# One more token-tile pair by seven half-size products in the first FFN, with the softmax steps set closer

## The chip, the cores and the metric

The kernel runs on one core of one Trainium2 chip. The metric is device time in microseconds, median of several runs. TensorE (PE) multiplies, VectorE (DVE) and ScalarE (ACT) work on SBUF and PSUM, GpSimd (POOL) on SBUF, SyncE (SP) issues every DMA.

## The reference

Attention over keys and values pooled by eight, then two feed-forward networks on 4608 tokens. All in float32.

```python
def _attn_ref(q, k, v):                        # 8 batches, 8 heads, 576 tokens, 64 wide
    k_p = k.reshape(B, H, Sp, pool, D).mean(axis=3)     # Sp = 72
    v_p = v.reshape(B, H, Sp, pool, D).mean(axis=3)
    scores = scale * np.matmul(q, k_p.transpose(0, 1, 3, 2))
    scores = scores - np.max(scores, axis=-1, keepdims=True)
    attn = np.exp(scores)
    attn = attn / (np.sum(attn, axis=-1, keepdims=True) + 1e-09)
    return np.matmul(attn, v_p)

def _moe_ref(x, w_in, w_out):                  # x: 4608 x 512, w_in: 512 x 2048
    h = x @ w_in
    return np.maximum(0.01 * h, h) @ w_out

def _moe2_ref(x, w_gate, w_val, w_out, rms_g): # 512 x 1536
    rms = np.sqrt(np.mean(x * x, axis=-1, keepdims=True) + 1e-06)
    xn = x / rms * rms_g
    g = xn @ w_gate
    return (g / (1.0 + np.exp(-g)) * (xn @ w_val)) @ w_out
```

## The kernel before

**Numbers.** Every factor of a large product is kept as a high and a low part, and a product is three matmuls (high by high, high by low, low by high). A result in PSUM is therefore read twice on its way to SBUF: ACT copies the high part, DVE or POOL subtracts it for the low part.

**Order.** Each engine executes its instructions in the order of the program text: at the end the kernel ties each instruction to the one before it on its engine. So the text is the schedule, and SP's queue of DMAs is one list too.

**Token tiles.** The 4608 tokens are nine tiles of 512. `PLAIN` of them, seven, go through the first FFN plainly: for each of 16 blocks f, `h_half` computes x@w_in in two chunks of six matmuls (192 matmuls in a tile); after the second chunk ACT applies the leaky ReLU twice (`h_high`) and DVE subtracts (`h_low`); two blocks later `y_unit` multiplies with w_out in two more chunks. From the third block on the chunks go h, h, y, y. A tile has 64 chunks, called stages here. Tile 0 has a hand-written order (`FIRST`) in which the attention of the first two batches and the preparation of the weights are laid out; its last 28 chunks are stages 0 to 27, tile 1 begins with stage 28.

**The pair.** The last two tiles are a pair: x@w_in goes by seven half-size products instead of eight (Strassen and Winograd's form; `Quad`, eight quads of seven products of six matmuls, `kinds` 1). Its operands are sums of halves of w_in, prepared earlier and stored to DRAM ("h" units), and of halves of x, made by `token_steps` from x in DRAM. Pieces of the product with w_out run between the products. The second FFN goes by pairs of the same kind throughout (`kinds` 2).

**Softmax steps.** After each chunk `attention_point` runs what `late_attention` put at that stage. Query tile i (batch b, tile t of five; the fifth has 64 new rows, the others 128) starts at `start[i]`. Its chain, and what stands behind it on the other engines:

```python
stage("s", b, t, (s, s, s + 1, s + 1, s + 3, s + 4))
stage("r", b, t, (s + 6,))
stage("x", b, t, (s + 7,) * 3)
stage("y", b, t, (s + 8,) * 3)
if i + 1 < len(tiles):
    stage("t", *tiles[i + 1], (s + 6,) * 2)
```

"s" is the scores in two halves (L322, tile `sc`; at s and s+1), on DVE their maximum and the subtraction (L335, L336), the exponential on ACT at s+3, the normalization on DVE at s+4 (last: L346). "x" transposes the exponentials (L383, `xt`), ACT copies the high part (L387), DVE subtracts (L389, `at`). "y" does so for the remainder that doesn't fill 128 rows (L397, `xr`; L401; L404, `atr`), "t" transposes the next queries (L302, `qt`). Transposes, scores and the products with v (`av`, L426, two stages behind the second and the fifth tile of a batch, one head pair per stage) share two PSUM banks, tag "att", handed out in turn. Within a stage what an earlier query tile put comes first.

**Where the output goes.** `step_av` writes the attention output of a plain tile to SBUF as high and low parts; that of the paired tiles is copied on ACT (L452, `xs`) and stored to DRAM two stages later. A chunk of 256 or 320 tokens that crosses a tile edge takes two copies.

**Side units.** The operands for the pairs and for the second FFN are built by units placed at stages (`side_steps`: 16 "h" units every `H_STEPS` stages from `SIDE_BEGIN` on, then gate, value and output units until `SIDE_END`); those left over run in the pair, one tick after each product or piece.

Of the kernel before, what the change touches and what calls it, by code (L numbers as in the profile page):

```python
# [9 lines left out]
F32 = mybir.dt.float32  # L10
# [13 lines left out]
def pooled_attention_then_two_ffns(  # L24
# [27 lines left out]
    N = 512  # L52
    NJ = NT // N
    begun = len(nc.cur_bb.bb.instructions)
    PLAIN = NJ - 2
    H_STEPS, G_STEPS, P_STEPS, SIDE_BEGIN, SIDE_END = 4, 11, 9, 84, 356
    QT = [0, 128, 256, 384, S - P]
    RB = [0, 128, 256, 384, H * SP - P]
    CH = [(0, 256, (0, 1)), (256, S, (2, 3, 4))]
# [350 lines left out]

    def x_tile(j):
        if j not in xhl:
            if j in (3, 6):
                xhl[j] = [weight_slot(9 + 2 * c, f"xhl{j}_{c}") for c in range(KC)]
            else:
                t = per.tile([P, 2, KC, N], F32R, tag="xhl", bufs=2, name=f"xhl{j}")
                xhl[j] = [t[:, :, c, :] for c in range(KC)]
        return xhl[j]
# [89 lines left out]
    def late_attention():  # L508

        def put(point, f):  # L510
            at_point.setdefault(point, []).append(f)

        def stage(kind, b, t, points):
            for point in points:
                put(point, lambda: go(kind, b, t))
            if kind in use:
                def free():
                    live["q" if kind == "t" else "kv"] -= 1
                put(points[0] + 3, free)

        start = {}
        for i in range(FIRST_LATE, len(tiles) + 1):
            start[i] = 34 + round(10.5 * (i - 10)) if i < 26 else 202 + 9 * (i - 26)
        for r, point in enumerate((4, 9, 14, 29, 31)):
            stage("kp", 2, r, (point,))
        stage("kt", 2, 0, (28,) * 2)
        stage("kt", 2, 1, (34,) * 2)
        stage("t", 2, 0, (28,) * 2)
        for i in range(FIRST_LATE, len(tiles)):
            b, t = tiles[i]  # L530
            s, after = start[i], start[i + 1]
# [6 lines that stand above are left out]
            if t < 2:  # L538
                for k in range(3):
                    stage("vp", b, 3 * t + k, (s + 2 * k,) * 2 + (s + 2 * k + 2,) * 2)  # L540
            if t in (2, 3) and b + 1 < B:
                for k in range(3 if t == 2 else 2):
                    stage("kp", b + 1, 3 * (t - 2) + k, (s + 4 * (t - 2) + 2 * k,))
                stage("kt", b + 1, t - 2, (after + 3,) * 2)
            if t in (1, 4):
                for p in range(NP):
                    stage(f"av{t // 4}", b, p, (after + 2 + p,) * 3)

    point_now = [0]
# [28 lines left out]
    for at_, (m, f) in enumerate(needs):  # L578
        src = rows(w_out, f) if m == "o" else cols(w_in, f)
        n = 2 * f + (m == "o")  # L580
# [3 lines left out]
    late_end = max(at_point) + 1  # L584
# [393 lines left out]
    def pair_loads(q):  # L978

        n = pairs[q][1]  # L980
        xs = [[None] * KC for _ in range(2)]

        def load(z, k):
            x = slot("u", 8 + 2 * z + k, f"xst{q}_{z}_{k}").bitcast(F32)
            j = pairs[q][0] // N + z
            nc.sync.dma_start(out=x, in_=x_dram[j][:, 2 * k:2 * k + 2, :])
            for c in range(2):
                xs[z][2 * k + c] = x[:, c, :]

        return xs, [lambda z=z, k=k: load(z, k) for z in range(2) for k in range(2)]  # L990
# [69 lines left out]
    def token_steps(q, xs, fine):  # L1060

        n = pairs[q][1]
        if kinds[q] == 2:
            xs = [[x[:, c, :] for c in range(KC)] for x in xs]
        t = tok[q] = {}
        box = {}
        done = [0]

        def parts(dst, src):
            done[0] += 1  # L1070
            split(nc.scalar, dst[:, HI, :], nc.gpsimd if done[0] % 3 == 0 else nc.vector, dst[:, LO, :], src)

        def sub(out, u, w):
            nc.vector.tensor_tensor(out=out, in0=u, in1=w, op=ALU.subtract)

        def first(c):
            if c == 0:
                box["a"] = per.tile([P, 2, KC, N], F32R, tag="xhl", bufs=2, name=f"xa{q}")
            t["B11", c] = box["a"][:, :, c, :n]
            t["B21", c] = box["a"][:, :, 2 + c, :n]  # L1080
            parts(t["B11", c], xs[0][c])

        def t_slot(name, c):
            i = {"T2": 0, "T1": 2, "T3": 4}[name] + c
            t[name, c] = slot("t", i, f"{name}_{q}_{c}")[:, :, :n]
            return t[name, c]

        def sums(c):
            a1, a2, b1, b2 = (xs[z][i] for z in range(2) for i in (c, 2 + c))
            for x in ("T3", "T2"):  # L1090
                box[x, c] = e_tile(n, f"{x}_{q}_{c}") if kinds[q] == 1 else (
                    per.tile([P, N], F32, tag="tg", bufs=3, name=f"{x}_{q}_{c}")[:, :n]
                )
            t3, t2 = box["T3", c], box["T2", c]
            sub(t3, b2, b1)
            sub(b1, b1, a1)
            sub(t2, b2, b1)

        def second(c):
            parts(t_slot("T2", c), box["T2", c])  # L1100
            parts(t_slot("T1", c), xs[1][c])

        def second_more(c):
            a2 = xs[0][2 + c]
            parts(t["B21", c], a2)
            parts(t_slot("T3", c), box["T3", c])
            sub(a2, a2, box["T2", c])

        def third(c):
            if c == 0:  # L1110
                box["b"] = per.tile([P, 2, KC, N], F32R, tag="xhl", bufs=2, name=f"xb{q}")
            t["T4", c] = box["b"][:, :, 2 + c, :n]
            t["B22", c] = box["b"][:, :, c, :n]
            parts(t["T4", c], xs[0][2 + c])
            parts(t["B22", c], xs[1][2 + c])

        def all_second(c):
            for f in (sums, second, second_more):
                f(c)

        two = (0, 1)
        early = [lambda c=c: first(c) for c in two]
        for c in two:
            early += [lambda c=c, f=f: f(c) for f in ((sums, second, second_more) if fine else (all_second,))]
        return early, [lambda c=c: third(c) for c in two]
# [70 lines left out]
    def first_pair(put):  # L1196
# [4 lines left out]
            put(i, x)  # L1201
        for i, x in zip((25, 27, 29, 31, 33, 36, 38, 41), early):
            put(i, x)
        for i, x in zip((44, 47), late):
            put(i, x)
        for i in (34, 36, 39, 41, 42, 44, 46, 48, 50, 52):
            put(i, load_a)
# [6 lines left out]
    def e_tile(n, name):  # L1214
        return p2.tile([P, N], F32, tag="e", bufs=9, name=name)[:, :n]
# [254 lines left out]
    n = 0  # L1470
# [10 lines left out]
    for j in range(1, PLAIN):  # L1481
        at_spot = {}
        last = j == PLAIN - 1
        if last:
            assert point_now[0] >= late_end
            begin_phase2()

        def put(i, x):
            at_spot.setdefault(i, []).append(x)
# [27 lines left out]
        if not last:  # L1517
            y_store(j)


    def piece():
        if pieces:
# [172 lines left out]
```

## Time and profile before

| | |
|---|---|
| median of 3 runs | 1790.53 us (1787.62 to 1790.8) |
| profiled execution | 1790.44 us, its span 1788.7 us |
| mean granted TensorE clock | 0.995 |
| PE busy | 1745.8 us, 98% of the span, 8488 matmuls |
| DVE, ACT, POOL busy | 913.4, 705.4, 624.6 us |
| tile 0, from the span's start | to about 169 us |
| plain tiles 1 to 5 | 169.02 to 705.91 us |
| plain tile 6 | 705.91 to about 787 us |
| the pair's products of x@w_in | 787.51 to 910.43 us |

Busy time of PE is the time between a matmul's start and its modelled end, which overlaps the next start: PE's pace is read from starts, and its waits from the gaps, which come out somewhat short. PEld is the weight load ahead of a matmul; a wait for a semaphore stands on it.

### The profile page before, as it was taken

What the parts mean: (1) busy time and instruction counts of PE and PEld (TensorE: products, weight loads), DVE (VectorE), ACT (ScalarE), POOL (GpSimd) and SP (SyncE); (2) the same over time, 40 slices, a digit from 0 to 9 for tenths busy, and PEclk for the clock granted to TensorE, in tenths of its full rate; (3) what the DMA queues carried; (4) which work ended last, traced back from release to release, by engine and by line L of the source; (5) the groups of instructions that cost most, each with busy time, mean ns of one, the idle gap of its engine ahead of it and who ended that gap; (6) DMA issues with size and microseconds to landing.
All of it is one profiled execution on the core that took longest, in us unless ns stands there. A gap on an engine that the chain in (4) does not pass through costs nothing.

```text
span 1788.7 us, 23981 instructions
## 1 busy us (share of the span) xinstructions
PE 1745.8 (98%) x8488; PEld 1484.2 (83%) x8488; DVE 913.4 (51%) x1610; ACT 705.4 (39%) x1512; POOL 624.6 (35%) x773
## 2 busy tenths in 40 slices
PE   5799999999999999999999999999999999999999
PEld 4689888888888888888788888999788889978887
DVE  7984447664655652335665445345534534553331
ACT  5664334454454543335453332243233223322220
POOL 5631317552434311114345332243144215413320
PEclk9899999999999999999999999999999999999999
DMA  8542655656566655659997656777765668676552
GB/s 250 184 154 96 250 193 182 192 181 209 165 213 204 188 155 176 202 182 381 311 311 256 217 197 227 238 278 251 256 235 195 216 225 302 241 256 212 181 209 93
DMA packets 203639, 387.46 MB, mean 217 GB/s; under 512 B 57216, under 2 KB 108416, under 8 KB 203008
## 3 DMA queue, kind: packets, MB, share of 16 engines
q1 hardware_dynamic: 203520, 385.94, 63.8%
q8 instruction: 67, 1.10, 0.3%
q14 instruction: 52, 0.43, 0.1%
HBM read 311.43 MB, written 74.45 MB: 216 GB/s over the span
## 4 chain that ended last, share of the span: by engine, by line
PE 89%; DVE 4%; DMA 3%; ACT 1%; issue 1%; POOL 1%; SPq 1%; ACTq 0%; POOLq 0%; DVEq 0%
PE o L1363 16%; PE y L641 16%; PE h L596 15%; PE yg L1235 6%; PE yv L1235 6%; PE o L1343 4%; PE xg L1235 4%; PE xv L1235 4%; PE wg L1235 4%; PE wv L1235 4%; PE sc L322 2%; PE yh L1235 1%; PE av L426 1%; PE wh L1235 1%; PE xh L1235 1%
## 5 line engine op out<-in xcount | busy, mean ns | idle before, releaser
L596 PE MATMUL h<-xhl,w_i 128*128 128x512 f32 (+1 forms) x1380 | 345.4, 393 | 8.0 <-DVE ghl L619 5.7
L1363 PE MATMUL o<-wo,u 128*128 128x512 f32 x1296 | 316.3, 392 | 3.1 <-DMA wo<-wo 3.0
L596 PEld LDWEIGHTS h<-xhl,w_i 128*128 128x128 f32 x1380 | 247.8, 190 | 53.1 <-DVE ghl L619 6.2
L1363 PEld LDWEIGHTS o<-wo,u 128*128 128x128 f32 x1296 | 243.3, 189 | 52.5 <-DMA wo<-wo 3.8
L619 DVE TENSOR_TENSOR ghl<-h,ghl 128x512 fp32r<-128x512 f32 (+1 forms) x115 | 77.8, 676 | 203.1 <-ACT h L101 197.1
L641 PE MATMUL y<-ghl,w_o 128*128 128x512 f32 (+1 forms) x864 | 174.3, 349 | 0.0
L641 PE MATMUL y<-ghl,wr 128*128 128x512 f32 x672 | 171.6, 397 | 0.0
L641 PEld LDWEIGHTS y<-ghl,w_o 128*128 128x128 f32 x864 | 136.5, 191 | 17.0
L641 PEld LDWEIGHTS y<-ghl,wr 128*128 128x128 f32 x672 | 122.4, 188 | 22.8
L101 ACT ACTIVATE ghl<-h 128x512 fp32r<-128x512 f32 (+1 forms) x115 | 67.4, 586 | 183.5 <-PE h L596 178.9
L98 POOL TENSOR_TENSOR u<-e2g,u 128x512 fp32r<-128x512 f32 (+1 forms) x25 | 29.6, 1184 | 304.9 <-ACT u L95 304.9
L1235 PE MATMUL yg<-T,ag 128*128 128x512 f32 (+1 forms) x360 | 84.0, 368 | 0.0
L1235 PE MATMUL yv<-T,av 128*128 128x512 f32 (+1 forms) x360 | 83.8, 368 | 0.0
L1235 PE MATMUL xg<-xa,ag 128*128 128x512 f32 (+1 forms) x360 | 83.8, 367 | 0.0
L1235 PE MATMUL xv<-xa,av 128*128 128x512 f32 (+1 forms) x360 | 83.7, 367 | 0.0
L1235 PEld LDWEIGHTS yg<-T,ag 128*128 128x128 f32 x360 | 66.0, 188 | 10.0 <-DVE e1v L1212 0.6
L1235 PEld LDWEIGHTS yv<-T,av 128*128 128x128 f32 x360 | 66.2, 188 | 9.5
L1235 PEld LDWEIGHTS xv<-xa,av 128*128 128x128 f32 x360 | 66.0, 188 | 9.5
L1235 PEld LDWEIGHTS xg<-xa,ag 128*128 128x128 f32 x360 | 66.1, 188 | 9.3
L228 POOL TENSOR_TENSOR v<-v 128x256 f32<-128x256 f32 (+1 forms) x96 | 63.6, 663 | 13.7 <-DMA v<-in_v_dram 10.0
L101 ACT ACTIVATE h<-h 128x512 f32<-128x512 f32 (+1 forms) x115 | 67.0, 582 | 0.0
L95 ACT ACTIVATE u<-e2g 128x512 fp32r<-128x512 f32 (+1 forms) x30 | 17.7, 590 | 120.6 <-DVE e2g L1266 120.6
(204 smaller groups left out, 3134.9 us busy)
## 6 DMA issues: line engine op xcount, KB each, us to landing
wo<-wo SPq DMA_DIRECT2D x148, 512.0 KB
ag<-op_g SPq DMA_DIRECT2D x90, 512.0 KB
av<-op_v SPq DMA_DIRECT2D x90, 512.0 KB
wr<-wo SPq DMA_DIRECT2D x56, 512.0 KB
k<-in_k_dram SPq DMA_DIRECT2D x40, 256.0 KB
q<-in_q_dram SPq DMA_DIRECT2D x40, 256.0 KB
op_g<-parts_g SPq DMA_DIRECT2D x36, 256.0 KB
op_v<-parts_v SPq DMA_DIRECT2D x36, 256.0 KB
```

Of the source, the lines that this page charges most:

```text
L95: nc.scalar.activation(out=hi, in_=src, func=AF.Copy)
L98: lo_eng.tensor_tensor(out=lo, in0=src, in1=hi.bitcast(F32), op=ALU.subtract)
L101: return nc.scalar.activation(out=out, in_=in_, func=AF.Prelu, scale=scale, alpha=alpha)
L228: nc.gpsimd.tensor_tensor(out=x[:, :n], in0=x[:, :n], in1=x[:, n:2 * n], op=ALU.add)
L322: nc.tensor.matmul(pt[:, i * n:(i + 1) * n], y[:, p, :], kblk[b % 2][:, p * n:(p + 1) * n], start=True, stop=True,)
L426: nc.tensor.matmul(pt[:, :n], vb[b, p][:, sp].rearrange("p h d -> p (h d)"), a[:, p, mp, 0:n], start=i == 0, stop=False,)
L596: nc.tensor.matmul(pt, w[:, sp, c * P:(c + 1) * P], x[c][:, mp, c0:c1], start=c == 0 and i == 0, stop=c == KC - 1 and i == 2,)
L619: nc.vector.tensor_tensor(out=t[:, LO, :], in0=pt, in1=t[:, HI, :].bitcast(F32), op=ALU.subtract)
L641: nc.tensor.matmul(pt, w[:, sp, m * P:(m + 1) * P], g[:, mp, a - c0:a - c0 + n], start=ydone[j, a] == 1 and i == 0 and m % per_bank == 0, ...
L1235: nc.tensor.matmul(pt, wt[:, a, c, sp, :], xt[:, mp, :], start=start and c == 0 and i == 0, stop=c == 1 and i == 2, skip_group_check=not s ...
L1343: nc.tensor.matmul(pt, w[:, sp, m * P:(m + 1) * P], u[:, mp, :], start=f == blocks(q, z)[0] and i == 0, stop=f == blocks(q, z)[-1] and i == 2,
L1363: nc.tensor.matmul(pt, u[:, sp, m * P:(m + 1) * P], w[:, mp, :], start=f == 0 and i == 0, stop=f == F2 - 1 and i == 2,)
```

## The change

The plain tiles become five (`PLAIN = NJ - 4`), and tiles 5 to 8 two pairs. The loop over `pairs` and `kinds` makes two pairs of kind 1 from that without further edits. Softmax steps now start every 7.9 stages, rounded: 26 of the 29 distances are 8, three are 7 (from (3,0), (4,4) and (7,0)); the last step's chain ends at stage 276 of 280. The h units come every six stages, the tile stages take 21 side units instead of 36, and 31 instead of 16 run in the pairs. x of the second pair is loaded into other slots; tile 4's x lies where tile 1's lay, so the splits that need the first pair's second x buffer stand at stages 58 and 59 of tile 4; two sums of the first pair use another pool, since the second phase's pool opens only behind the last plain tile.

```diff
--- before.py
+++ after.py
@@ -52,8 +52,8 @@
     N = 512
     NJ = NT // N
     begun = len(nc.cur_bb.bb.instructions)
-    PLAIN = NJ - 2
-    H_STEPS, G_STEPS, P_STEPS, SIDE_BEGIN, SIDE_END = 4, 11, 9, 84, 356
+    PLAIN = NJ - 4
+    H_STEPS, G_STEPS, P_STEPS, SIDE_BEGIN, SIDE_END = 6, 11, 9, 84, 228
     QT = [0, 128, 256, 384, S - P]
     RB = [0, 128, 256, 384, H * SP - P]
     CH = [(0, 256, (0, 1)), (256, S, (2, 3, 4))]
@@ -410,7 +410,7 @@
 
     def x_tile(j):
         if j not in xhl:
-            if j in (3, 6):
+            if j == 3:
                 xhl[j] = [weight_slot(9 + 2 * c, f"xhl{j}_{c}") for c in range(KC)]
             else:
                 t = per.tile([P, 2, KC, N], F32R, tag="xhl", bufs=2, name=f"xhl{j}")
@@ -520,7 +520,7 @@
 
         start = {}
         for i in range(FIRST_LATE, len(tiles) + 1):
-            start[i] = 34 + round(10.5 * (i - 10)) if i < 26 else 202 + 9 * (i - 26)
+            start[i] = 34 + round(7.9 * (i - 10))
         for r, point in enumerate((4, 9, 14, 29, 31)):
             stage("kp", 2, r, (point,))
         stage("kt", 2, 0, (28,) * 2)
@@ -981,7 +981,7 @@
         xs = [[None] * KC for _ in range(2)]
 
         def load(z, k):
-            x = slot("u", 8 + 2 * z + k, f"xst{q}_{z}_{k}").bitcast(F32)
+            x = slot("u", (6, 7, 2, 3)[2 * z + k] if q else 8 + 2 * z + k, f"xst{q}_{z}_{k}").bitcast(F32)
             j = pairs[q][0] // N + z
             nc.sync.dma_start(out=x, in_=x_dram[j][:, 2 * k:2 * k + 2, :])
             for c in range(2):
@@ -1088,7 +1088,7 @@
         def sums(c):
             a1, a2, b1, b2 = (xs[z][i] for z in range(2) for i in (c, 2 + c))
             for x in ("T3", "T2"):
-                box[x, c] = e_tile(n, f"{x}_{q}_{c}") if kinds[q] == 1 else (
+                box[x, c] = e_tile(n, f"{x}_{q}_{c}") if kinds[q] == 1 and q else (
                     per.tile([P, N], F32, tag="tg", bufs=3, name=f"{x}_{q}_{c}")[:, :n]
                 )
             t3, t2 = box["T3", c], box["T2", c]
@@ -1201,7 +1201,7 @@
             put(i, x)
         for i, x in zip((25, 27, 29, 31, 33, 36, 38, 41), early):
             put(i, x)
-        for i, x in zip((44, 47), late):
+        for i, x in zip((58, 59), late):
             put(i, x)
         for i in (34, 36, 39, 41, 42, 44, 46, 48, 50, 52):
             put(i, load_a)
@@ -1481,9 +1481,6 @@
     for j in range(1, PLAIN):
         at_spot = {}
         last = j == PLAIN - 1
-        if last:
-            assert point_now[0] >= late_end
-            begin_phase2()
 
         def put(i, x):
             at_spot.setdefault(i, []).append(x)
@@ -1518,6 +1515,9 @@
             y_store(j)
 
 
+    assert point_now[0] >= late_end
+    begin_phase2()
+
     def piece():
         if pieces:
             pieces.pop(0)()
```

## Rows read from the trace of the kernel before

**Rows 1.** The page's first part: busy time, share of the span, instructions of each engine.

```profile
PE 1745.8 (98%) x8488; PEld 1484.2 (83%) x8488; DVE 913.4 (51%) x1610; ACT 705.4 (39%) x1512; POOL 624.6 (35%) x773
```

**Rows 2.** Windows: us; busy PE, PEld, DVE, ACT, POOL (count); granted clock; DMA share; GB/s.

```profile
169.02:705.91 536.89, 534.04 (x2684) 445.92 (x2683) 289.64 (x629) 243.67 (x615) 208.50 (x353) 1.00 0.60 196
274.37:381.98 107.61, 106.34 (x532) 88.07 (x531) 73.67 (x167) 50.12 (x121) 69.19 (x103) 1.00 0.65 199
...
705.91:787.51 81.60, 81.60 (x361) 67.59 (x360) 28.22 (x42) 28.65 (x56) 10.63 (x12) 1.00 0.59 195
787.51:910.43 122.92, 120.47 (x527) 98.44 (x526) 69.88 (x124) 59.65 (x120) 42.98 (x49) 1.00 0.89 313
```

**Rows 3.** Timeline of PE in the pair: start, us, engine, line, operation, names, shapes, count.

```profile
848.70 1.52 PE L1235 MATMUL xh<-xa,ah 128*128 128x512 f32 x6
...
854.14 1.52 PE L1235 MATMUL yh<-T,ah 128*128 128x512 f32 x6
```

**Rows 4.** Timeline around the step of query tile (6,2), in tile 4.

```profile
566.08 0.60 PE L383 MATMUL xt<-ident,ex 128*128 128x128 f32 x4
...
567.40 0.69 DVE L389 TENSOR_TENSOR at<-xt,at 128x512 fp32r<-128x512 f32 x1 [2.75 <-ACT at L387]
...
568.05 1.64 PE L596 MATMUL h<-xhl,w_i 128*128 128x512 f32 x6
...
569.52 0.66 PE L322 MATMUL sc<-kblk,qT 128*128 128x144 f32 x4
...
569.92 1.41 PE L641 MATMUL y<-ghl,wr 128*128 128x512 f32 x5
```

**Rows 5.** Timeline around the step of query tile (6,3), in tile 4.

```profile
580.66 1.02 DVE L346 TENSOR_TENSOR ex<-ex,st 128x576 f32<-128x576 f32 x1
...
581.83 0.63 PE L383 MATMUL xt<-ident,ex 128*128 128x128 f32 x4 [0.74 <-DVE ex L346]
...
583.17 0.69 DVE L389 TENSOR_TENSOR at<-xt,at 128x512 fp32r<-128x512 f32 x1 [1.49 <-ACT at L387]
...
583.83 1.64 PE L641 MATMUL y<-ghl,w_o 128*128 128x512 f32 x6
...
585.30 0.66 PE L322 MATMUL sc<-kblk,qT 128*128 128x144 f32 x4
...
585.73 0.42 DVE L404 TENSOR_TENSOR atr<-xr,atr 32x256 fp32r<-32x256 f32 x1
```

**Rows 6.** Timeline around the step of query tile (6,0), in tile 4.

```profile
537.09 0.68 DVE L389 TENSOR_TENSOR at<-xt,at 128x512 fp32r<-128x512 f32 x1
...
537.13 1.63 PE L641 MATMUL y<-ghl,wr 128*128 128x512 f32 x6
```

**Rows 7.** Timeline of DVE at the scores of (6,3).

```profile
573.13 0.46 DVE L336 TENSOR_TENSOR ex<-sc,st 128x288 f32<-128x288 f32 x1
```

**Rows 8.** Waits of PE in tile 0 (36 to 169 us): total, times, longest.

```profile
PE av L426 <- DVE at L389: 2.7, 1, 2.7
...
PE sc L322 <- DVE at L389: 0.6, 1, 0.6
```

**Rows 9.** Waits of PE in tiles 1 to 5, longest total first.

```profile
PE xt L383 <- DVE ex L346: 1.2, 3, 0.7
```

**Rows 10.** Timeline where batch 7 crosses the edge of tiles 7 and 8.

```profile
639.37 1.56 PE L641 MATMUL y<-ghl,wr 128*128 128x512 f32 x6
640.95 0.46 ACT L452 COPY xs<-av 128x64 f32<-128x64 f32 x2 [4.67 <-DMA x<-xs]
...
641.46 0.62 PE L426 MATMUL av<-at,vb 128*128 128x256 f32 x3 [0.54 <-ACT xs L452]
```

**Rows 11.** Waits of PE in the pair's quads (787.51 to 910.43 us).

```profile
PE ms L1035 <- ACT ahl L95: 1.5, 1, 1.5
PE yh L1235 <- DVE e7h L1212: 0.6, 1, 0.6
```

**Rows 12.** Windows in the second FFN, columns as in rows 2.

```profile
1580.00:1590.00 10.00, 7.83 (x28) 5.99 (x27) 7.64 (x10) 4.95 (x10) 3.70 (x3) 0.83 0.70 226
```

## The prediction

> **What bounds the kernel now.** First the page's busy line: TensorE (PE) is busy 1745.8 of 1788.7 us, VectorE (DVE) 51%, ScalarE (ACT) 39%, GpSimd (POOL) 35% [rows 1]. Then the windows by token tile, since a share over the whole span hides stages: tiles 1 to 5 take 536.89 us, of which PE idles 2.85, and tile 6, without softmax work, not at all [rows 2]. So PE sets the time of the stretch that the change touches, and only two things can move it: how many matmuls PE runs, and how often it waits in its program order for another engine. For the pace, tile 6's 360 matmuls of 512 columns in 81.60 us are 226.7 ns each (the window counts one that hangs over) [rows 2].
>
> **What is removed.** Two plain tiles run 2 x 192 matmuls of x@w_in; the pair that exists now runs 56 half-size products of six, 336, at the same pace: 24 matmuls start between 848.70 and 854.14 [rows 3]. Nothing else on PE changes: the second product keeps 2 x 192, the softmax its transposes and scores. One more pair is therefore 48 matmuls less, 48 x 226.7 ns = 10.88 us. Of all terms this one is sure.
>
> **What is squeezed, as throughput.** The softmax of 30 query tiles is spread over five plain tiles now and must fit into four, about 536.89 - 384 x 0.2267 = 449.8 us. Even if all work of the other engines in the five tiles came along, DVE would be at 289.64/449.8 = 64%, ACT at 54%, POOL at 46%. Tile 2 runs today with DVE at 73.67/107.61 = 68% and PE idle 1.3 us [rows 2]. The side units only ease it (the h units come every six stages instead of four, 15 units move into the pairs). So no engine becomes the bound by its sum, and I cost density itself at nothing; what PE pays is single waits.
>
> **What is squeezed, as distance.** A step of query tile i starts at stage s; the transposes of its exponentials (xt) stand at s+7, those of their remainder (xr) at s+8, the scores of tile i+1 at the next s, in two halves a stage apart. All of them, and the query transposes (qt, at s+6), take turns in the two "att" banks in the order qt, xt, xr, scores 1, scores 2. So scores 1 reuse the bank of xt and wait for its last reader, the DVE subtraction of line 389. Steps are 9 to 11 stages apart now and 8 (three times 7) after. At 9, two chunks of six matmuls lie between xt and scores 1; at 8 only one.
>
> In an ordinary step xt ends at 566.68 and the subtraction at 567.40 + 0.69 = 568.09. Scores 1 come at 569.52 now; at a distance of 8 they are due right behind xr, where the next chunk starts now, at 568.05 [rows 4]. A release takes 0.15 us more (a normalization ends at 581.68, the transposes that waited for it start at 581.83 [rows 5]). They start at 568.24, 0.19 late. Eleven full-width steps, (5,0) to (5,3), (6,0) to (6,3) and (7,1) to (7,3), will lie so: 2.1 us.
>
> Where the chunk ahead of xt ends an h block, its two PReLUs go first on ACT and its own subtraction first on DVE. Then line 389 ends at 537.77 where the scores would be due at 537.13 [rows 6]: with the release 0.79 late. Steps that start at stages 34 to 58 fall so (s+7 is the second half of an h block): four full-width ones, 3.2 us.
>
> From stage 81 to 137 it is xr that stands behind the PReLUs, and scores 2 reuse its bank. In such a step, where xr stands just ahead of the chunk at 583.83, its subtraction ends at 586.15. At a distance of 8 scores 1 are due at 583.83 and, by line 389 (583.17 + 0.69), start 0.18 late; scores 2 are due one score group (0.40, as behind 569.52) and one chunk (1.47) later, at 585.88, and start at 586.30: 0.42 late [rows 4, 5]. Seven such steps at 0.60, and (3,4), whose narrow transposes leave only the second wait, 0.4: 4.6 us.
>
> Three steps are 7 apart. There scores 2 reuse the bank of scores 1, whose two DVE operations (0.46 each [rows 7]) stand behind line 389: 1.41 + 0.92 + 0.15 after xt against some 1.75 due, 0.7 late, and up to 0.8 more behind PReLUs. Estimate 3.0 together, 1 to 4.5. The narrow fifth tiles (2,4), (5,4) and (6,4) I take as free.
>
> Sum 12.9 us. No row of tiles 1 to 5 shows this wait; the nearest are in tile 0, where scores waited 0.6 and a product 2.7 us for the same subtraction [rows 8]. So a single wait lies between 0 and 2.7; I take the values above because they come from today's own end times.
>
> **Other terms.** (a) Stages 81 to 145 also put an h block's subtraction ahead of the normalization, which then ends just before xt, once 0.74 us too late [rows 5]. Steps in that position go from five to nine; today's waits there sum to 1.2 us [rows 9], so +1.0 (0 to 3). (b) Attention output of tiles 5 and 6 now goes to DRAM and back. Where a chunk of tokens crosses a tile edge, the copies of the second head pair wait on ACT until the first pair's stores have landed: ACT stood 4.67 us, and PE's next product, due 1.36 us after 639.37, came at 641.46, 0.73 late [rows 10]. One such crossing now, three after: +1.5 (0 to 9.3, if all of ACT's wait reached PE). (c) The new pair repeats the pair's wait for a sum: +0.6 [rows 11]. Its norm waits stay with the pair ahead of the second FFN. (d) The loads of x, the splits at stages 58 and 59 (needed seven products and pieces, about 9 us, later) and the late units are covered: the pair keeps one late unit per 8 or 5 ticks, as now, and PE never waits for DMA there at a DMA share of 0.89 [rows 2, 11]. If that cover fails, the nearest price is an idle stretch in the second FFN: 2.2 of 10 us, and 1.7 more, since the granted clock was 0.83 over them [rows 12].
>
> That also bears on the waits above: idle stretches of 0.7 and 1.5 us left the granted clock at 1.00 [rows 2, 5, 11], and the one of 2.2 us brought a stretch at the lower level (1.2 of 2.4 GHz). So I add nothing for the clock. The Trainium skill (TensorE: Matmul & The Clock Gate, A second HAM failure mode: psum-queue depth-cycling) has it otherwise: small idles from cycling through PSUM banks can come so often that the clock swings between its levels. By that rule the sum would grow by the rival below; by the rows it does not.
>
> **Total.** 1790.44 (profiled execution; the median of the runs is 1790.53) - 10.88 + 12.9 + 1.0 + 1.5 + 0.6 = **1795.6 us**, 0.3% slower.
>
> **Rivals.** *The gain stands.* If the scratch banks don't bind, only (a) to (c) remain: 1790.44 - 10.88 + 3.1 = 1782.7. It decides whether line 389 ends within 1.2 us of xt; it takes 1.41 today, so a small misreading decides much. For it: PE waits for no score in tiles 1 to 5. Against it: the distances there are longer by a chunk or more. *It cancels.* The waits of 0.19 and 0.18 vanish (3.4 us), (a) and (b) cost nothing, the longer ones remain: 16.0 - 5.9 = 10.1 against 10.88, 1789.7. *The clock follows.* If the seven or so longest waits (behind PReLUs, at distance 7) each bring a stretch at the lower level, 1.7 us each, 12 more: 1808. Against it: the idles that did not. The skill's section named above is what speaks for it. *The queues pile up*: the pair's sums, splits and loads fall into tile 4 beside softmax work; the forecast's upper end, to 1802.
>
> **Chances.** What a measurement of this kernel can tell from no change is about 0.2%, 3.6 us. The forecast with its own range, 1794 to 1802: 0.48; clock or DMA beyond it: 0.04; it cancels (1787 to 1794): 0.28; the gain stands (1780 to 1787): 0.20. So slower 0.52, same 0.28, faster 0.20. Leaving out the clock and most of the gaining case gives a range of 1783 to 1802.
>
> **What would show it.** The two pairs' x@w_in should run 336 matmuls each, at 227 ns. In tiles 1 to 4 the PE waits should have scores waiting for DVE "at" (line 389) and, from stage 81 to 145, for "atr" (line 404), in nearly every step, with a PE idle of some 15 us in four tiles where five had 2.85; "av" should wait for ACT "xs" three times; the clock should stay at 1.00. The forecast is wrong if those tiles show PE idle under 6 us: then the bank order or the release time was misread. If they show it and the time still falls, the pairs gave back more than 48 matmuls.

## The result and the profile after

The changed kernel takes 1814.31 us (median of four runs, 1813.02 to 1816.15), the kernel before 1790.66 beside it: ratio 1.0134, 95% interval 1.0117 to 1.0152, 1.3% slower. The profiled execution has a span of 1812.9 us against 1788.7, 24.2 more, where the sum had 5.1.

The page's busy line and the windows by stage of the changed kernel (columns as in [rows 2]): tiles 1 to 4, the first pair's quads, its second half, and the second pair.

```profile
PE 1748.3 (96%) x8440; PEld 1480.3 (82%) x8440; DVE 937.2 (52%) x1633; ACT 720.8 (40%) x1539; POOL 650.6 (36%) x797
```

```profile
169.06:284.99 115.93, 111.98 (x571) 92.64 (x569) 55.08 (x119) 46.86 (x125) 43.40 (x88) 1.00 0.60 213
284.99:408.33 123.34, 117.73 (x592) 95.85 (x591) 71.56 (x167) 54.18 (x141) 58.23 (x95) 0.99 0.52 159
408.33:524.41 116.08, 114.50 (x594) 95.44 (x593) 67.11 (x144) 56.21 (x145) 55.08 (x97) 1.00 0.64 201
524.41:637.34 112.93, 105.92 (x528) 87.67 (x526) 59.05 (x112) 52.74 (x131) 24.73 (x41) 0.98 0.58 186
637.34:755.79 118.45, 118.41 (x523) 97.74 (x521) 55.03 (x107) 52.96 (x109) 37.03 (x47) 1.00 0.91 307
755.79:810.44 54.65, 48.68 (x201) 39.10 (x200) 34.49 (x45) 24.31 (x49) 26.48 (x23) 0.94 0.86 304
810.44:978.00 167.56, 164.26 (x722) 134.99 (x721) 107.07 (x171) 85.83 (x171) 75.23 (x78) 1.00 0.89 304
```

PE runs 48 matmuls less, 8440 for 8488 [rows 1], so the gain of 10.9 us is there, and it is lost more than three times over. Six tiles took 618.49 us before [rows 2]; two of them at 384 x 226.7 ns are 174.1, which would leave 444.4 for four. They take 468.28 (169.06 to 637.34): **23.9 us lost** where the sum had 15.4. The pair before took 167.79 (787.51 to 955.30), and one more at the pace of its matmuls is 720 x 0.2267 = 163.2; the two take 173.10 + 167.56: **9.7 us lost**, nearly all in the first pair's second half, where the sum had 0.6. The second FFN behind them takes 1.5 more. 23.9 + 9.7 + 1.5 - 10.9 = 24.2.

PE idles 18.15 us in tiles 1 to 4, 2.85 in tiles 1 to 5 before [rows 2]. Its waits there (total, times, longest), to be held against [rows 9]:

```profile
PE sc L322 <- DVE at L389: 9.4, 12, 2.7
PE xt L383 <- ACT xs L452: 3.1, 2, 2.8
PE xt L383 <- DVE ex L346: 1.8, 3, 0.9
PE qt L302 <- ACT xs L452: 0.9, 1, 0.9
PE sc L322 <- DVE ex L336: 0.9, 2, 0.5
PE av L426 <- ACT xs L452: 0.7, 1, 0.7
```

The wait that no row of before's tiles showed, scores for the subtraction of line 389, is now the first. One of the twelve, from the timeline of the changed kernel in tile 1 (step of query tile (2,0)):

```profile
190.64 0.60 PE L383 MATMUL xt<-ident,ex 128*128 128x128 f32 x4
...
190.90 0.60 ACT L101 ACTIVATE ghl<-h 128x512 fp32r<-128x512 f32 x1 [0.66 <-PE h L596]
...
191.39 0.59 ACT L101 ACTIVATE h<-h 128x512 f32<-128x512 f32 x1
...
191.91 0.59 ACT L387 ACTIVATE at<-xt 128x512 fp32r<-128x512 f32 x1
192.02 0.69 DVE L619 TENSOR_TENSOR ghl<-h,ghl 128x512 fp32r<-128x512 f32 x1 [1.20 <-ACT h L101]
...
192.62 0.68 DVE L389 TENSOR_TENSOR at<-xt,at 128x512 fp32r<-128x512 f32 x1
...
193.36 0.76 PE L322 MATMUL sc<-kblk,qT 128*128 128x144 f32 x4 [0.51 <-DVE at L389]
```

The h block that ends ahead of xt puts two PReLUs (L101) ahead of the copy L387 on ACT and L619 ahead of L389 on DVE. L389 ends at 193.30, 2.0 us behind xt; the scores, one chunk and the remainder behind xt, wait for it. In a step without PReLUs the same pair ends 1.4 us behind xt. Seven of the twelve waits stand behind PReLUs in this way, 2.9 of the 9.4 us. At the other five, 6.4 us, side work stands ahead of L389 on ACT or DVE: a unit's conversion or the preparation of v (waits of 1.19, 2.70 and 0.75 us, at 280.66, 357.23 and 575.21) and the first pair's token sums (0.83 and 0.96 us, at 597.02 and 611.32; at 597.02 an h block's subtraction too). DVE ahead of the last one:

```profile
608.70 1.36 DVE L98 TENSOR_TENSOR T<-T,T 128x512 fp32r<-128x512 f32 x1 [0.37 <-ACT T L95]
...
609.99 0.68 DVE L1074 TENSOR_TENSOR xst<-xst,T 128x512 f32<-128x512 f32 x1
610.59 0.68 DVE L389 TENSOR_TENSOR at<-xt,at 128x512 fp32r<-128x512 f32 x1
```

The longest waits, PE's rows at four places of the timeline:

```profile
357.23 1.33 PE L322 MATMUL sc<-kblk,qT 128*128 128x144 f32 x4 [2.70 <-DVE at L389]
...
592.42 1.12 PE L383 MATMUL xt<-ident,ex 128*128 128x128 f32 x4 [2.78 <-ACT xs L452]
...
777.66 1.62 PE L1343 MATMUL o<-ug,wo 128*128 128x512 f32 x3 [3.80 <-DMA wo<-wo]
...
807.80 2.80 PE L1343 MATMUL o<-ug,wo 128*128 128x512 f32 x11 [1.42 <-POOL ug L98]
```

and what the clock did behind the first three, with the end of the first pair as the fourth row (windows):

```profile
357.20:361.00 3.80, 3.77 (x15) 3.30 (x15) 3.33 (x8) 0.63 (x1) 3.64 (x7) 0.61 0.45 125
592.40:596.00 3.60, 3.58 (x12) 2.89 (x12) 2.58 (x3) 3.33 (x8) 1.33 (x1) 0.54 0.08 27
777.60:784.00 6.40, 6.34 (x16) 5.04 (x17) 0.12 (x1) 0.78 (x2) 0.83 (x2) 0.54 1.04 412
795.00:810.44 15.44, 13.28 (x58) 10.33 (x57) 14.67 (x14) 7.77 (x16) 12.43 (x10) 1.00 0.72 243
```

Each of the three is followed by a stretch at or near the lower level (1.2 of 2.4 GHz). At a granted clock of 0.61 a stretch of 3.80 us does the work of 2.32, so it costs 1.5 us; the others 1.7 and 2.9: by this estimate about 6 us in all, 3 of them in the tiles. It is an upper bound: in runs 3, 4 and 12 below the same wait in tile 2 (2.69 us) left the clock at 1.00, and tile 2 takes only 0.6 to 0.8 us less (122.72, 122.71 and 122.58 for 123.34). In the fourth row DVE is busy 14.67 of 15.44 us: the next pair's token splits and the late units meet there, and ug comes late.

At 592.42 the cause is an edge crossing. ACT's wait for stores in tiles 1 to 4:

```profile
ACT xs L452 <- DMA x<-xs: 17.8, 10, 4.9
```

### The profile page after: what moved, and what is told of

Read it like the earlier page. It is cut to its first block, busy times and chain, and to the rows that moved or that the text cites. A ratio compares the mean times of both kernels' runs of the same rounds, so it can differ in the third digit from the quotient of the medians.

```text
span 1812.9 us, 24130 instructions
## 1 busy us (share of the span) xinstructions
PE 1748.3 (96%) x8440; PEld 1480.3 (82%) x8440; DVE 937.2 (52%) x1633; ACT 720.8 (40%) x1539; POOL 650.6 (36%) x797
## 4 chain that ended last, share of the span: by engine, by line
PE 79%; DVE 7%; DMA 5%; ACT 3%; issue 3%; POOL 1%; SPq 1%; POOLq 0%; ACTq 0%; DVEq 0%
PE o L1363 16%; PE h L596 8%; PE y L641 8%; PE o L1343 7%; PE yg L1235 6%; PE yv L1235 6%; PE xg L1235 4%; PE xv L1235 4%; PE wg L1235 4%; PE wv L1235 4%; PE yh L1235 3%; PE wh L1235 2%; DMA v<-in_v_dram 2%; PE xh L1235 2%; PE sc L322 2%
## 5 line engine op out<-in xcount | busy, mean ns | idle before, releaser
L596 PE MATMUL h<-xhl,w_i 128*128 128x512 f32 (+1 forms) x996 | 249.9, 393 | 6.9 <-DVE ghl L619 5.5
L596 PEld LDWEIGHTS h<-xhl,w_i 128*128 128x128 f32 x996 | 176.9, 190 | 37.6 <-DVE ghl L619 6.0
L641 PE MATMUL y<-ghl,w_o 128*128 128x256 f32 (+1 forms) x768 | 151.7, 344 | 0.0
L619 DVE TENSOR_TENSOR ghl<-h,ghl 128x512 fp32r<-128x512 f32 (+1 forms) x83 | 55.6, 670 | 124.5 <-ACT h L101 124.5
L641 PE MATMUL y<-ghl,wr 128*128 128x512 f32 x384 | 101.8, 405 | 0.0
L1343 PE MATMUL o<-ug,wo 128*128 128x512 f32 x384 | 92.4, 399 | 6.0 <-DMA wo<-wo 3.8
L1343 PE MATMUL o<-u,wo 128*128 128x512 f32 x384 | 96.2, 389 | 0.0
L1343 PEld LDWEIGHTS o<-ug,wo 128*128 128x128 f32 x384 | 73.7, 193 | 23.0 <-issue 4.2
L101 ACT ACTIVATE ghl<-h 128x512 fp32r<-128x512 f32 (+1 forms) x83 | 48.3, 582 | 99.6 <-PE h L596 93.7
L1343 PEld LDWEIGHTS o<-u,wo 128*128 128x128 f32 x384 | 72.1, 188 | 14.9
L641 PEld LDWEIGHTS y<-ghl,wr 128*128 128x128 f32 x384 | 70.9, 193 | 12.8
L322 PE MATMUL sc<-kblk,qT 128*128 128x144 f32 x320 | 60.0, 316 | 15.5 <-DVE at L389 9.9
```

The lines of the kernel that those rows point to most:

```text
L101: return nc.scalar.activation(out=out, in_=in_, func=AF.Prelu, scale=scale, alpha=alpha)
L322: nc.tensor.matmul(pt[:, i * n:(i + 1) * n], y[:, p, :], kblk[b % 2][:, p * n:(p + 1) * n], start=True, stop=True,)
L596: nc.tensor.matmul(pt, w[:, sp, c * P:(c + 1) * P], x[c][:, mp, c0:c1], start=c == 0 and i == 0, stop=c == KC - 1 and i == 2,)
L619: nc.vector.tensor_tensor(out=t[:, LO, :], in0=pt, in1=t[:, HI, :].bitcast(F32), op=ALU.subtract)
L641: nc.tensor.matmul(pt, w[:, sp, m * P:(m + 1) * P], g[:, mp, a - c0:a - c0 + n], start=ydone[j, a] == 1 and i == 0 and m % per_bank == 0, ...
L1343: nc.tensor.matmul(pt, w[:, sp, m * P:(m + 1) * P], u[:, mp, :], start=f == blocks(q, z)[0] and i == 0, stop=f == blocks(q, z)[-1] and i == 2,
```

## The experiments

**Theory at the start:** at distances of 8 the two scratch banks come round too early for their readers (*banks*); the crossings' stores, and the late units in the first pair's second half, cost the rest. **Rival:** the softmax of five tiles in four is too much for ACT and DVE where it falls, so that any single wait taken away comes back at another product (*backlog*). Times are set against 1814.31 for kernels built on the changed one, and against the kernel before in the same job (1790.2 to 1791.2) for the others.

**1. Xr ahead of xt.**

```diff
+            stage("y", b, t, (s + 7,) * 3)
             stage("x", b, t, (s + 7,) * 3)
-            stage("y", b, t, (s + 8,) * 3)
```

> The changed kernel with the transposes of the remainder (xr) issued at stage s+7 just ahead of xt instead of at s+8 behind it; same work, same density, same distance of steps. The scratch banks then go round as qt, xr, xt, scores 1, scores 2: scores 1 reuse the bank of xr, whose reader is short and goes first, and scores 2 that of xt, a stage later. Theory of the banks: the waits of scores for the subtraction of line 389 (9.4 us in 12 in tiles 1 to 4 of the changed kernel, some 15 us with what they delay) vanish or fall below 3 us, and the time falls by 11 to 15 us, to 1799 to 1803. Rival, backlog: the softmax of four tiles is simply too dense for VectorE and ScalarE, so that the wait only moves to another product (xt or av waiting for its exponentials or copies); then the time stays at 1810 to 1816.

Measured: 1815.35 us, ratio 1.0142 (1.0126 to 1.0157): nothing gained. Waits of PE in its tiles 1 to 4 (the longest two rows):

```profile
PE xr L397 <- ACT er L374: 9.1, 7, 5.1
PE sc L322 <- DVE atr L404: 7.0, 11, 2.2
```

Scores no longer wait for L389, but for L404, which stands behind the same PReLUs at an h block's end; and the remainder, now earlier, waits for ACT's copy of its own exponentials. But 5.1 of its 9.1 us are one wait, at 593.19: there that copy stands on ACT behind the attention copies of an edge crossing, which wait for stores. It is the wait of 592.42 in the changed kernel at another product. In both senses the rival is right here: the waits moved.

**2. Near steps in the kernel before.**

```diff
             start[i] = 34 + round(10.5 * (i - 10)) if i < 26 else 202 + 9 * (i - 26)
+        for i, s in zip((10, 12, 14, 16, 18, 20, 22, 24, 26, 30, 34, 38),
+                        (34, 54, 74, 98, 118, 138, 158, 182, 202, 238, 274, 310)):
+            start[i], start[i + 1] = s, s + 8
```

> The kernel before, with twelve of its query-tile steps moved so that twelve distances between steps are 8 stages and the next ones correspondingly longer; number of steps per tile, side units and everything else as before, so the mean density is unchanged. Theory of the banks: twelve scores wait for line 389, where there were none, 0.2 to 0.8 us each, and the time grows by 5 to 9 us, to 1796 to 1800 (ratio 1.003 to 1.005). Rival, density: without more work per tile nothing changes, 1789 to 1793.

Measured: 1801.21 us, ratio 1.0056 (1.0044 to 1.0069), 10.3 us more, above the 5 to 9 expected. Waits of PE in tiles 1 to 5, where [rows 9] had none of this kind:

```profile
PE sc L322 <- DVE at L389: 8.9, 11, 2.8
```

So distance alone, with no more work per tile, makes this wait: the mean density is not what does it. Nearly each of the twelve steps shows it.

**3. One store tile at an edge.**

```diff
+        whole = None
...
-                if p < 2:
-                    x = ap.tile([P, CHMAX], F32, tag="xs", bufs=2, name=name)[:, :t1 - t0]
-                else:
-                    x = per.tile([P, N], F32, tag="tg", bufs=3, name=name)[:, :t1 - t0]
+                if whole is None and p < 2:
+                    whole = ap.tile([P, CHMAX], F32, tag="xs", bufs=2, name=name)
+                elif whole is None:
+                    whole = per.tile([P, N], F32, tag="tg", bufs=3, name=name)
+                x = whole[:, t0 - b * S - c0:t1 - b * S - c0]
```

> The changed kernel with one SBUF tile for each head pair's attention output also where its chunk of tokens crosses a tile edge (two spans of one tile, two stores) instead of one tile for each span, so that the second head pair's copies no longer wait for the first pair's stores. Theory of the edge crossings: ScalarE's wait for stores (17.8 us in 10 in tiles 1 to 4) goes to near zero, and with it TensorE's 2.8 us at 592 and the stretch at the lower clock behind it: 5 to 8 us less, 1806 to 1809. Rival: ScalarE has slack there and TensorE's waits are those for the banks, which stay: 1812 to 1816.

Measured: 1810.68 us, ratio 1.0112 (1.0098 to 1.0126), 3.6 us less by the medians, below the range given and with an interval that touches the changed kernel's. In the traces tiles 1 to 4 are 5.0 us shorter, 2.9 of it in tile 4; ACT's wait for stores falls from 17.8 to 3.3 us, and PE's wait at 592 is gone. The lower clock there is not: in tile 4 of this run it stands behind two waits of 0.81 and 1.30 us (at 588.36 and 590.09).

**4. No late units in the first pair's second half.**

```diff
-                    ((0, 13), (1, 15)), G_STEPS, 8,
+                    ((0, 13), (1, 15)), G_STEPS, 7,
...
-                tick()
+                if q:
+                    tick()
                 continue
```

> The changed kernel without late side units (weight conversion for the second FFN) in the second half of the first pair; they run in the two pairs' quads and the second half of the other pair, with one step less between them (7 for 8) so that they still end in time. Theory: the late units' transfers ahead of wo on SP's queue and their work on GpSimd beside VectorE's token splits make the waits for wo (3.8 us), ug (2.1) and e6h (2.6) and the lower clock (0.94 in that stretch): 5 to 9 us less, 1805 to 1809. Rival: the loads of x and the splits of the next pair do it by themselves, or the units only move the wait into pair 1: 1811 to 1816.

Measured: 1809.71 us, ratio 1.0100 (1.0085 to 1.0114), 4.6 us less, just short of the 5 to 9 expected. The windows of that second half and of the next pair's quads:

```profile
757.74:803.31 45.57, 45.55 (x201) 37.21 (x200) 27.14 (x33) 20.80 (x40) 18.70 (x15) 1.00 0.83 280
803.31:925.45 122.14, 117.72 (x511) 96.41 (x510) 76.99 (x131) 62.14 (x126) 52.16 (x59) 0.99 0.91 317
```

The second half takes 45.57 for 54.65, with PE busy throughout and the clock at 1.00: 9.1 us that the late units cost there. Some of it comes back, 1.4 us in the first pair's quads and 2.5 in the second's, where the units run now. Tiles 1 to 4, which the edit doesn't touch, are 2.0 us longer in this trace than in the changed kernel's (470.23 for 468.28): so much can differ between two traces.

**5. Xr behind the next scores.**

```diff
             stage("s", b, t, (s, s, s + 1, s + 1, s + 3, s + 4))
+            if i > FIRST_LATE:
+                stage("y", *tiles[i - 1], (s + 1,) * 3)
...
-            stage("y", b, t, (s + 8,) * 3)
+            if i + 1 == len(tiles):
+                stage("y", b, t, (s + 8,) * 3)
```

> The changed kernel with the remainder's transposes (xr) issued one stage later, right behind scores 2 of the next query tile, so that the two scratch banks go round as qt, xt, scores 1, scores 2, xr. Scores 1 then reuse the bank of qt, which they need done anyway, and scores 2 that of xt a chunk and a score group later; the remainder is not pulled ahead of its own exponentials, as it was in the run with xr ahead of xt, where the wait went to the remainder itself (9.1 us in 7). Steps are as near to each other as in the changed kernel and the work is the same. Theory of the banks: scores wait for line 389 under 2 us in tiles 1 to 4 and the time falls by 10 to 15 us, to 1799 to 1804. Rival, backlog: the wait only moves, to xr or av, and the time stays at 1810 to 1816.

Measured: 1810.25 us, ratio 1.0109 (1.0095 to 1.0122): 4.1 us less, not 10 to 15. Waits in tiles 1 to 4, and one of them in the timeline:

```profile
PE xr L397 <- DVE ex L336: 5.9, 9, 2.3
...
PE sc L322 <- DVE at L389: 1.2, 2, 1.1
```

```profile
291.93 0.69 DVE L622 TENSOR_TENSOR ghl<-h,ghl 128x512 fp32r<-128x512 f32 x1 [1.18 <-ACT h L101]
...
293.02 0.46 DVE L336 TENSOR_TENSOR ex<-sc,st 128x288 f32<-128x288 f32 x1
...
293.62 0.40 PE L397 MATMUL xr<-ident,er 128*96 128x128 f32 x2 [0.53 <-DVE ex L336]
```

Tile 1, whose steps have xt behind an h block, is 5.0 us shorter. In tiles 2 and 3 (1.9 and 1.5 longer) the PReLUs fall elsewhere: the h block's subtraction (L622 there, L619 of the changed kernel), itself late by 1.18 us because DVE waits for ACT's PReLUs, now delays the readers of scores 1, and xr (in tile 3 the products with v) waits for their bank. Whatever comes next in the banks waits for DVE at that place.

**6. The PReLUs behind the stage's softmax work.** The two runs above point at the order on ACT and DVE, not at the banks' order.

```diff
         if cs[-1] == KC - 1 and j:
-            h_high(j, f, c0)
-            h_low(j, f, c0)
+            behind.append(lambda: (h_high(j, f, c0), h_low(j, f, c0)))
...
             attention_point()
+            while behind:
+                behind.pop(0)()
```

> The changed kernel with the two PReLUs and the subtraction of an h block issued behind the softmax work of the same stage instead of ahead of it; nothing else moves. By the theory of the banks the subtraction of line 389 then ends 1.4 us behind xt in the steps at an h block's end too, where it ends 2.0 to 2.8 us behind it in the changed kernel: some twelve waits fall from about 0.7 to 0.1 us, and the time by 4 to 8 us, to 1806 to 1810. If the waits come from how much work ScalarE and VectorE have rather than from its order, 1812 to 1816.

Measured: 1801.64 us, ratio 1.0059 (1.0047 to 1.0072), 12.7 us less: more than expected, from order alone. The step (2,0) again:

```profile
191.40 0.60 PE L383 MATMUL xt<-ident,ex 128*128 128x128 f32 x4
...
192.04 0.60 ACT L387 ACTIVATE at<-xt 128x512 fp32r<-128x512 f32 x1 [1.04 <-PE xt L383]
192.53 0.59 ACT L101 ACTIVATE ghl<-h 128x512 fp32r<-128x512 f32 x1
192.67 0.69 DVE L389 TENSOR_TENSOR at<-xt,at 128x512 fp32r<-128x512 f32 x1 [1.08 <-ACT at L387]
...
193.45 0.72 PE L322 MATMUL sc<-kblk,qT 128*128 128x144 f32 x4
```

L389 ends 1.36 us behind xt's end (192.00) and the scores start without a wait. The waits that are left, in tiles 1 to 4:

```profile
PE sc L322 <- DVE at L389: 5.1, 5, 1.9
PE xt L383 <- ACT xs L452: 3.1, 2, 2.8
```

Tile 1 is 4.2 us and tile 2 is 9.5 us shorter; in tile 2 the wait of 2.70 and its stretch at the lower clock went too. Tiles 3 and 4 gain nothing: the five waits for L389 that are left stand behind side work or the PReLUs of the stage before.

Not all of this can be laid to PReLUs ahead of L389: the wait of 2.70 has none there. L274 at 353.35 in the changed kernel, its cause, took 3.09 to 3.13 us in each of the seven kernels that have the near steps without edit 6 (the changed one, runs 1, 3, 4, 5, 7 and 12), and 0.99 to 1.35 in the three with it (runs 6, 8 and 10). So part of tile 2's 9.5 us comes with the shorter L274; how much, and why it is shorter, was not separated.

**7 and 8. Together.** Edits 3, 4 and 5; then those and edit 6.

> Xr behind the next scores, one store tile where a chunk of tokens crosses an edge, and no late units in the first pair's second half, together on the changed kernel: the three causes that the trace gave for the loss. If they are separate causes, the gains add: 12 and 4 and 5 us off, 1791 to 1796. If the first two remove the same waits, or the clock's swings come back elsewhere, 1798 to 1806.

> As the kernel with the three causes taken away, and the PReLUs of an h block issued behind the softmax work of their stage. With the banks freed by the order alone, the place of the PReLUs should matter little for scores and something for the normalizations that end just before xt: 0 to 4 us less than that kernel, 1788 to 1795. It beats the kernel before (1790.7) only if nearly all waits of tiles 1 to 4 are gone; the floor by the matmuls alone, with the waits for normalizations and edges that the kernel before has too, is about 1780 to 1783. Rival: the late PReLUs make the second product wait for its h block: 1796 or more.

Measured: 1797.1 us, ratio 1.0036 (1.0022 to 1.0050), and 1781.38 us, ratio **0.9947 (0.9935 to 0.9960)**: with all four the change is 9.7 us faster than the kernel before. Run 7 lies between its two expectations, just above the one for separate causes (1791 to 1796); run 8 lies below its own (1788 to 1795). Waits of PE in tiles 1 to 4 of the last one:

```profile
PE xr L397 <- DVE ex L336: 1.5, 4, 0.8
PE xt L383 <- DVE ex L346: 0.6, 1, 0.6
PE sc L322 <- DVE at L389: 0.2, 1, 0.2
```

Its tiles 1 to 4 take 443.4 us (169.54 to 612.89), the 444.4 that two tiles less should leave. Density, then, costs nothing, and *backlog* is out: the same softmax and side work runs in the same four tiles.

**9 to 11. What belongs to what:** edit 6 on the kernel before, edits 3, 4 and 6 without 5, and edit 6 on run 2.

> The kernel before with the PReLUs of an h block issued behind the softmax work of the same stage. Its steps are 9 to 11 stages apart, and in tiles 1 to 5 PE waits 2.6 us in all. If the place of the PReLUs counts only where the steps are near, as the theory of the banks has it, the time is 1788 to 1791 (0 to 2.5 us less). Rival: ScalarE's order costs the kernel before as well, beyond its recorded waits, and the gain of the changed kernel with all four causes undone does not belong to the pairs: 1780 to 1787.

> The kernel with all four causes undone (1781.4), but with xr at its old place, so that scores 1 reuse the bank of xt again. If the gains add (PReLUs 12.7, store tiles 3.6, late units 4.6 off 1814.3): 1793 to 1795, and the order of the banks is worth some 12 us of its own once the PReLUs are out of the way. If the place of the PReLUs was the whole cause of the scores' waits: 1781 to 1785.

> The kernel before with twelve distances of 8 between its steps (10.3 us more than the kernel before) and with the PReLUs of an h block issued behind the softmax work of the stage. The twelve steps have their xt behind an h block or their xr behind the PReLUs. Theory: the bank is reused at once only because line 389 stands behind the PReLUs' work; 6 to 10 us of the 10.3 go, to 1791 to 1795. Rival: the distance alone does it, whatever the order on ScalarE and VectorE: 1798 to 1802.

Measured: 1789.55 us, ratio 0.9992 (0.9984 to 1.0001); 1787.61 us, ratio 0.9975 (0.9965 to 0.9985); 1793.58 us, ratio 1.0018 (1.0010 to 1.0027). With steps 9 to 11 apart the place of the PReLUs does not matter; with twelve steps 8 apart it takes back 7.6 of 10.3 us, and in the uneven run of the eleven waits three are left, all behind a unit's conversion or the preparation of v:

```profile
PE sc L322 <- DVE at L389: 2.5, 3, 1.5
```

The order of the banks is worth 6.2 us more (1787.61 to 1781.38; 5.0 by the ratios) once the PReLUs are out of the way, half of the 12 that adding the gains gave: run 10 falls between its two expectations. So for most of the loss two things had to meet: a bank that comes round one chunk behind its product, and readers that stand behind other work, the PReLUs above all in the uneven run. Where side work stands there instead, 3.0 us of such waits are left in run 10, and 0.2 with the banks reordered too (run 8).

**12. Which part of the late units?**

```diff
-                tick()
+                if q or i > 8:
+                    tick()
                 continue
```

> The changed kernel, whose late units pause only in the first nine steps of the first pair's second half, where the next pair's four loads of x are issued, and go on in the rest of it. Theory of the transfers: wo came 3.8 us late because the loads of x and the units' loads and stores stand ahead of it on SP's queue, and the lower clock behind it is that wait's; then the wait for wo and the lower clock go, the waits for ug (0.7 and 1.4 us) stay, and the first pair's second half takes 46 to 49 us instead of 54.7: 5 to 8 us less, 1806 to 1809. Rival, the engines: the units' conversions beside the token splits make the loss; then the waits stay or move with the units, and the time is 1811 to 1816.

Measured: 1809.4 us, ratio 1.0118 (1.0095 to 1.0140), between the two expectations and not to be told from the changed kernel. The second half, 755.58 to 808.03, takes 52.45 us. Its windows where wo was waited for, behind that, and at the end:

```profile
771.00:779.00 8.00, 5.50 (x24) 4.20 (x23) 0.69 (x1) 1.26 (x2) 1.35 (x2) 0.95 0.93 352
779.00:787.00 8.00, 8.00 (x31) 6.49 (x30) 2.50 (x4) 3.50 (x7) 3.12 (x3) 0.84 0.94 343
...
795.00:808.03 13.03, 10.70 (x46) 8.20 (x45) 12.68 (x11) 6.86 (x15) 11.36 (x9) 1.00 0.78 268
```

The wait for wo is still there, 2.50 us, and the clock still falls behind it; at the end DVE is still busy 12.68 of 13.03 us. Either the pause was too short or the queue was already behind by then; no run tells. That the late units make the loss is shown by run 4; by which of their parts (transfers, SP's order, or conversions) stays open.

## Why the prediction was right or wrong

**The matmuls** (-10.88) were right: 48 less, and two pairs whose undisturbed quads run at the old pace (523 matmul records in 118.45 us).

**Density costs nothing, distance does**: right. DVE is busy 252.79 of 468.28 us in tiles 1 to 4 (54%), run 2 makes the wait without density, and run 8 has the density without the wait.

**The score waits** (12.9): right in place and kind, near in size, wrong in what makes them. In tiles 1 to 4 PE's gaps ahead of scores sum to 10.8 us, and gaps come out somewhat short; PE's idle of 18.15 us is near the 15 forecast. But the "ordinary" waits of 0.19 are hardly in the trace, and the four steps that I priced at 0.79 behind PReLUs wait 0.44 to 0.51. Two of the eleven steps that I took for ordinary, (5,0) and (6,3), have PReLUs ahead of L389 too (0.45 each). Two thirds of the wait for L389, 6.4 of 9.4 us, stand behind side work, for which I had no term. That the sum came near is therefore partly luck. I had measured the lateness of line 389 in the step behind PReLUs [rows 6] and still took it for a property of the distance; moving the PReLUs gave 12.7 us, as much as the whole term. The longest of these waits: at 357.23 the scores waited 2.70 us because a VectorE subtraction (L274) took 3.09 us, while one of the same shape took 0.42 at 351.70, and L389 came behind it.

```profile
353.35 3.09 DVE L274 TENSOR_TENSOR vb<-vm,vb 32x256 fp32r<-32x256 f32 x1 [1.24 <-ACT vb L272]
356.48 0.69 DVE L389 TENSOR_TENSOR at<-xt,at 128x512 fp32r<-128x512 f32 x1
```

Of the 19.1 us that the sum missed, 9.1 are in the first pair's second half, 8.5 in tiles 1 to 4 and 1.5 in the second FFN, whose waits grew from 3.0 to 3.7 us.

**The step that failed most is (d)**, "are covered: the pair keeps one late unit per 8 or 5 ticks, as now". The tick rate is the same, but what runs beside the units is not: the first pair's second half issues the four loads of x for the next pair, and by the code it packs the token splits into its steps from the twelfth on, where a pair ahead of the second FFN spreads them over every second step from the fourth. 9.1 us are lost there (run 4: 45.57 us for 54.65), where the sum had nothing and a failed cover was priced at 2.2 + 1.7.

**Term (b)**, the edges (1.5), was too small: 3.6 us by the medians of run 3, 5.0 by its trace. I took 0.73 from one crossing for all three. In tile 3 that is near: ACT stood 4.87 us in one wait, and PE waited 0.71 and 0.36. In tile 4 ACT stood 2.38, 1.95 and 2.35 us in a row, and PE waited 0.91 and 2.78. Why that crossing costs more was not tried.

**"I add nothing for the clock"** failed. The rows that I rested on were idles of up to 1.5 us, and in the changed kernel's tiles and pairs those leave the clock up too; what I did not see is that single waits of 2.7 to 3.8 us would come, behind L274, a store and wo, and these three bring up to 6 us at the lower clock. The rule of the Trainium skill (TensorE: Matmul & The Clock Gate, A second HAM failure mode: psum-queue depth-cycling) is not what happened in the changed kernel: the many small waits at the banks left the granted clock at 1.00 (tiles 1 and 3), and the swings stand behind single long ones. In run 3 one swing stands behind two shorter waits.

So "the clock follows" (1808) named the price but put it on the waits behind PReLUs, and "the queues pile up" named tile 4, where two score waits do stand behind the token sums, but not the second half, and with too low an end. (a) held: normalizations 1.8 us for 1.2 + 1.0. (c) was too small in its one wait, 2.57 us for a sum (818.75, behind a late unit's conversion) for 0.6, but the second pair as a whole takes no longer than the pair before (167.56 for 167.79).

On ACT and DVE at 45% and 54% busy with PE idle, the Trainium skill (Perfetto Trace Analysis, Optimizing Scalar/DVE Operations) says that breaking up instructions may help when engines that aren't saturated make bubbles elsewhere. The trace agrees with its premise; here no instruction was made smaller, and a change of order alone gave 12.7 us.

**Open:** the single gains of edits 3 to 6 add up to 25.0 us and together give 32.9. Some of the difference is within the intervals (about 2.5 us each); the rest stays open. One place shows in the traces: tile 4 takes 112.93 us in the changed kernel, 110.01, 110.92 and 113.20 with edits 3, 5 and 6 alone, each still with a stretch at the lower clock, and 105.09 with all of them, without one. Nor was it tried why L274 took 3.09 us; in the trace five POOL instructions run back to back beside it (352.83 to about 356.8).

## What to carry to other kernels

When steps move nearer, ask for each reused bank or buffer not only who reads it last but what stands ahead of that reader on its engine, and move that before touching the buffers: a reordering of the buffers alone sent the wait to the next product twice here, and gave 5 to 6 us once the readers were moved too. A stage that is copied is not covered because its model was: list what its new neighbour brings (loads, splits, stores) on the same queues. And a shortage that looks like density is tested by making the distances uneven at the same density.

## What was unexpected of the hardware

In the changed kernel's tiles and pairs, waits of PE up to 1.5 us left the granted clock at 1.00. Behind waits of 2.70, 2.78 and 3.80 us it was 0.50 in the next two microseconds; but behind one of 2.57 us (at 818.75, in the second pair's quads) and one of 2.78 us (at 302.72, in the uneven run) it stayed at 1.00. Neither the length of a wait nor its place decides it alone. The wait in tile 2 was 2.69 us in runs 3, 4 and 12, and the clock stayed up; in run 3:

```profile
356.97:358.97 2.00, 2.00 (x10) 1.53 (x10) 1.97 (x5) 0.56 (x1) 1.84 (x4) 1.00 0.84 227
```

The wait of 2.57 us for the same sum brought the lower level in run 5 (0.50 from 814.95 to 816.95). In run 3 the waits of 0.81 and 1.30 us in tile 4 were followed by 0.50 (592.09 to 594.09), and in the second FFN of the changed kernel one of 1.82 us was too (1289.42 to 1291.42). So whether one trace has such a stretch says little of an edit.
